# Attention pairs: one value half in a single run of four chunks, and full 128x128 transposes for the last keys and the tails of q and k

## The chip, the cores and the metric

The kernel runs on one core of one Trainium2 chip. The core has five engines that run at the same time and wait for each other by semaphores: TensorE (PE in the rows; its weight loads are PEld), VectorE (DVE), ScalarE (ACT), GpSimd (POOL) and SyncE (SP), which here issues the DMA transfers. The metric is the device time of one launch in microseconds (us); less is better.

## The reference

Three layers follow each other: an attention with a learned relative bias, a mixture of experts with one expert for each token, and a layer that takes the maximum of three projections. The change is in the first.

```
# q, k, v: (4 batches, 8 heads, 576 positions, 64)
scores = q @ k^T / sqrt(64) + bias[head]          # 576 x 576 for each batch and head
attn = exp(scores - max) / (sum + 1e-9)
x = attn @ v                                      # then (2304 tokens, 512) for the experts
out = max_of_three(experts(x))
```

All numbers are float32. Matmuls that need full precision use a high and a low part of each operand.

## The kernel before, in words

The 32 heads are worked on as 16 **pairs** of two heads, numbered here 0 to 15. The 576 queries of a head are four tiles of 128 and a **tail** of 64; the 576 keys are four chunks of 128 and the last 64. A pair takes five **steps**, 0 to 4. Steps 0 to 3 take one query tile of both heads each; step 4 takes the tails of both heads together.

The order in which instructions stand on each engine is the order in which the loop at the end of `attention` issues them; no scheduler moves them. In a step TensorE is given, in this order:

- the scores of this step (`scores`, L262): two products for each head, one that reads `qs` and `kh` and one that reads `qz` and `kl`;
- transposes that prepare a later pair (`prep`): its tails of q and k in step 0 (L176), its k in step 2 and its q in step 3 (L179); in some steps also a piece of work for the rows of a batch that is done (L425, L434, L445);
- a part of the product with the values (`av`, L409 and L405), into the one PSUM tile `oT`;
- the transposes of the probabilities that were normed one step before (`transpose_step`, L380 for the first 512 keys, L390 or L395 for the last 64).

The product with the values is made in two parts of the queries: j = 0 is the first 256 queries (steps 0 and 1), j = 1 the other 320. Table `AV` says which key chunks of which part stand in which step; chunk 4 is the last 64 keys of both heads in one full matmul (L405), the chunks 0 to 3 are two matmuls each, for one head on array columns 0 to 63 and for the other on 64 to 127.

The scores of the next pair need its q and k in a layout with both heads on all partitions. For that the transposed q is split into a high part by ScalarE (L194) and a low part by VectorE (L207), both in `hl`, and `move` issues six transfers on SP's queue: for each head two into `qs` (L216) and one into `qz` (L220). This stands in step 3; before them on the same queue, from step 2, stand four transfers into `kh` (L218) and two loads of a later k (L146). SP takes its queue strictly in order. The first use of `qs` and `qz` is in step 0 of the next pair, with step 4 between.

`norm_step` (L352 to L359) makes VectorE work out 1 over the sums, and GpSimd multiply the probabilities into `pr`. PSUM tiles of tag T (`pt`, `tp`, `tq` and others) share three buffers.

Of the kernel before, what the change touches and what calls it, by code (L numbers as in the profile page):

```python
# [12 lines left out]
F32 = mybir.dt.float32  # L13
# [4 lines left out]
ALU = mybir.AluOpType  # L18
# [4 lines left out]
P = 128  # L23
B, H, S, D = 4, 8, 576, 64
# [14 lines left out]
TAIL = S - 4 * P  # L39
# [57 lines left out]
def attention(tc, A, ident, x_dram, route, rpool, store):  # L97
    nc = tc.nc
    with ExitStack() as ctx:
# [4 lines left out]
        pl = ctx.enter_context(tc.tile_pool(name="pl", bufs=2, reuse_waits="tile"))  # L104
# [16 lines left out]
        HALF = (slice(0, D), slice(D, P))  # L121

        def load_pair(b, hp):

            t = {}
            for nm in ("q", "k"):
                t[nm] = pl.tile([P, 4, 2, D], F32, name=f"{nm}n", tag=f"{nm}n", bufs=1)
            t["tail"] = pl.tile([TAIL, 2, 2, D], F32, name="tn", tag="tn", bufs=1)
            t["v"] = pl.tile([P, 4, 2, D], F32, name="vn", tag="vn")


            t["qz"], t["vt"] = qz[hp % 2], vd[hp % 2]
            t["qs"] = pl.tile([P, 2, 512], F32R, name="qs", tag="qs")
            t["qd"] = qd[hp % 2]
            t["kh"] = pl.tile([P, 2, S], F32R, name="kh", tag="kh")
            t["kn"] = pl.tile([P, S], F32R, name="kn", tag="kn2")
            t["kl"] = pl.tile([P, S], F32R, name="kl", tag="kl")

            def load(nm):
                hs = slice(2 * hp, 2 * hp + 2)  # L140
                if nm == "tail":
                    for i, x in enumerate(("q", "k")):
                        nc.sync.dma_start(out=t[nm][:, i], in_=A[x][b, hs, 4 * P :].rearrange("h p d -> p h d"))
                    return
                for h in range(2):
                    nc.sync.dma_start(out=t[nm][:, :, h, :], in_=A[nm][b, 2 * hp + h, : 4 * P].rearrange("(c p) d -> p c d", p=P))  # L146
                if nm == "v":
                    for h in range(2):
                        nc.sync.dma_start(out=t["vt"][HALF[h], h, :], in_=A["v"][b, 2 * hp + h, 4 * P :])

            t["load"] = load
            return t

        st = [load_pair(*pairs[0])]
        mod = route.modality_rows()

# [15 lines left out]
        def prep(t, nm, pt):  # L172

            if nm == "tail":
                for i in range(2):
                    nc.tensor.transpose(pt[:, i * TAIL : (i + 1) * TAIL], t["tail"][:, i].rearrange("p h d -> p (h d)"), ident[:TAIL, :TAIL])  # L176
            else:
                for c in range(4):
                    nc.tensor.transpose(pt[:, c * P : (c + 1) * P], t[nm][:, c, :, :].rearrange("p h d -> p (h d)"), ident)  # L179
            return pt  # L180
# [130 lines left out]
        pTt = pb.tile([P, S], F32, name="pTt", bufs=1)  # L311
# [38 lines left out]
        def norm_step(mz, es):  # L350
            n = len(es)
            nc.vector.tensor_scalar(mz[:, 1, :n], mz[:, 1, :n], 1e-9, None, op0=ALU.add)  # L352
            nc.vector.reciprocal(mz[:, 1, :n], mz[:, 1, :n])
            pr = pb.tile([P, 2 * S], F32, name="pr", tag="pr", bufs=2)
            nc.gpsimd.tensor_scalar(pr[:, :S], es[0], mz[:, 1, 0:1], 1.0, op0=ALU.mult, op1=ALU.mult)  # L355
            if n == 2:
                r = mz[:, 1, 1:2]
                nc.gpsimd.tensor_scalar(pr[:, S : S + TAIL], es[1][:, 4 * P :], r, 1.0, op0=ALU.mult, op1=ALU.mult)
                nc.gpsimd.tensor_scalar(pr[:, S + TAIL :], es[1][:, : 4 * P], r, 1.0, op0=ALU.mult, op1=ALU.mult)  # L359
            return pr  # L360

        def ptile(t, h, it):
            if it < 2:
                return t["pT0"][:, h, :, it * P : (it + 1) * P]
            q = it * P - Q0
            return t["pT1"][:, h, :, q : q + (P if it < 4 else TAIL)]

        def transpose_step(t, it, pr):
            if it == 0:
                t["pT0"] = pb.tile([P, 2, 4, Q0], F32, name="pT0", tag="pT0", bufs=1)  # L370
                t["pTt"] = pTt
            if it == 2:
                t["pT1"] = pb.tile([P, 2, 4, Q1], F32, name="pT1", tag="pT1", bufs=1)
            for h in range(2):
                if it == 4 and h == 1:
                    break
                o = 0 if h == 0 else S + TAIL
                tp = ps.tile([P, 512], F32, name="tp", tag="T", bufs=3)
                for c in range(4):
                    nc.tensor.transpose(tp[:, c * P : (c + 1) * P], pr[:, o + c * P : o + (c + 1) * P], ident)  # L380
                if it < 4:
                    (nc.scalar.copy if h else nc.vector.tensor_copy)(ptile(t, h, it), tp.rearrange("p (c q) -> p c q", c=4))  # L382
                else:
                    for j in range(2):
                        (nc.scalar.copy if j else nc.vector.tensor_copy)(
                            ptile(t, j, it), tp.rearrange("p (c h q) -> p c h q", c=4, h=2)[:, :, j, :]
                        )
            tq = ps.tile([P, 512], F32, name="tq", tag="T", bufs=3)
            if it < 4:
                nc.tensor.transpose(tq[:, :P], pr[:, 4 * P : 4 * P + P], ident)  # L390
                nc.scalar.copy(t["pTt"][:, it * P : (it + 1) * P], tq[:, :P])
            else:
                for h in range(2):
                    hs = slice(h * D, h * D + D)
                    nc.tensor.matmul(tq[hs, :TAIL], pr[hs, 4 * P : S], ident[hs, hs], start=True, stop=True)  # L395
                nc.vector.tensor_copy(t["pTt"][:, 4 * P :], tq[:, :TAIL])

        def av(t, j, cs):
            if cs[0] == 0:
# [70 lines left out]

        PREP0 = ("tail", "k", "q", None, None)
        PREP = ("tail", None, "k", "q", None)
        AV = (((1, 0, (2, 3)),), ((1, 0, (4,)),), ((1, 1, (0, 1)),), ((1, 1, (2, 3, 4)),), ((0, 0, (0, 1)),))
        st = st + [None] * len(pairs)
        ROWS = (1, 2, 3, 4)
        LR = 4
# [11 lines left out]
        for i in range(len(steps) + 5):  # L488
            n, it = i // 5, i % 5
            cur = st[n] if n < len(pairs) else None  # L490
            last = st[n - 1] if n > 0 else None
            if cur:
                nm = (PREP if n else PREP0)[it]
                nxt = (st[n + 1], nm) if n + 1 < len(pairs) and nm else None
                mid = row_q and it in ROWS
                soft, pr = soft_step(cur, pairs[n][1], it, nxt, pend, row_q.pop(0) if mid else None, n >= len(pairs) - NP2, early.pop(0) if early else None)
            else:
                soft, pr = None, norm_step(*pend) if pend else None
            ready[i - 1] = pr
            pend = soft  # L500
            for back, j, cs in AV[it]:
                t = last if back else cur
                if t:
                    av(t, j, cs)
                    if 4 in cs:
                        evict_o(t, j)
            if 0 <= i - 2 < len(steps):
                m, jt = steps[i - 2]
                transpose_step(st[m], jt, ready.pop(i - 2))
            for f in EARLY.get((n, it), ()):  # L510
                f()
            if last and it == 3:
                b, hp = pairs[n - 1]
                if hp == NP2 - 1:
                    xTs = [st[n - NP2 + i2]["xT"] for i2 in range(NP2)]
                    if b == B - 1:
                        assert not ops
                        return lambda *allocs: batch_done(b, xTs, *allocs)
                    row_q += batch_done(b, xTs, talloc, lambda: px.tile([P, DM], F32, name="xr", tag="xr"))
            if n < len(pairs):  # L520
                if it == 0 and n + 2 < len(pairs):
                    st[n + 2] = load_pair(*pairs[n + 2])
                if it == 4 and n + 1 < len(pairs):
                    st[n + 1]["load"]("v")
                if nm and n + 2 < len(pairs):
                    st[n + 2]["load"](nm)
            if i > 7:
                next(gates, None)
            if i > 4:
                next(rconst, None)  # L530
# [1057 lines left out]
```

## Time and profile before

| what | value |
| --- | --- |
| median of 3 runs | 953.15 us (952.73 to 954.08) |
| the profiled execution | 953.03 us |
| its span, from first to last instruction | 951.3 us |
| TensorE busy | 923.9 us, 97% |
| VectorE, ScalarE, GpSimd busy | 547.5, 429.7, 206.3 us |

The profiled execution lies 1.7 us above its span and 0.1 us under the median. Matmuls are pipelined: a row's printed duration holds the time that a result needs to come out, so the cost of a group of matmuls on TensorE is read from its start to the start of the next group. Lines are those of the kernel before.

### The profile page before, as it was taken

How to read it: one execution, taken by the hardware profiler on the slowest of the kernel's cores; microseconds unless marked ns; L12 is line 12 of the kernel's file. 1: busy time of each engine (PE TensorE's matmuls, PEld its weight loads, DVE VectorE, ACT ScalarE, POOL GpSimd, SP SyncE). 2: the span in 40 equal slices, each digit the busy share in tenths (PEclk: the TensorE clock that was granted, in tenths of full speed). 3: DMA queues.
4: the chain of work that ended last, by engine and by line, in shares of the span. 5: the costliest groups of instructions: out<-in, count | busy, mean ns of one | idle time of the engine just before them, and what ended most of it. 6: DMA issues, size and time to landing. Idle time of an engine off the chain costs nothing. (4 is left out here: it accounts for less than half of the span.)

```text
span 951.3 us, 16953 instructions
## 1 busy us (share of the span) xinstructions
PE 923.9 (97%) x5667; PEld 723.8 (76%) x5667; DVE 547.5 (58%) x1267; ACT 429.7 (45%) x889; POOL 206.3 (22%) x350
## 2 busy tenths in 40 slices
PE   6989999999999999999999999999999999999996
PEld 3436777777777777788888887888888888888885
DVE  7976777877877886633355368525455365522221
ACT  6977766666767666322244256432111011122221
POOL 1004544453353451211112111110000000001112
PEclk9999999999999999999999999999999999999999
DMA  5976664664565564321234459314021121000111
GB/s 124 213 189 172 143 143 100 174 149 111 144 159 132 127 188 139 100 56 57 65 128 143 145 192 335 126 36 155 2 87 45 45 90 45 22 23 34 45 45 55
DMA packets 111037, 106.67 MB, mean 112 GB/s; under 512 B 69788, under 2 KB 79260, under 8 KB 110941
## 3 DMA queue, kind: packets, MB, share of 16 engines
q1 hardware_dynamic: 106140, 90.53, 34.7%
q0 software_dynamic: 4800, 14.97, 5.1%
q8 instruction: 47, 0.77, 0.4%
q14 instruction: 50, 0.40, 0.1%
HBM read 121.57 MB, written 14.96 MB: 144 GB/s over the span
## 5 line engine op out<-in xcount | busy, mean ns | idle before, releaser
L280 ACT ACTIVATE e<-e,mz 128x576 f32<-128x576 f32 x144 | 110.5, 770 | 34.4 <-DVE mz L268 34.4
L268 DVE CUSTOM_DVE_ANT_0 e<-s,bias 128x576 f32<-128x576 f32 x140 | 101.6, 756 | 18.1 <-PE s L262 17.0
L355 POOL TENSOR_SCALAR pr<-e,mz 128x576 f32<-128x576 f32 x80 | 59.7, 746 | 219.4 <-DMA bias<-ev 73.7
L380 PEld LDWEIGHTS tp<-ident,pr 128*128 128x128 f32 x576 | 64.0, 141 | 26.6 <-issue 10.0
L935 DVE TENSOR_TENSOR hl<-ht,hh 128x512 fp32r<-128x512 f32 x42 | 29.1, 692 | 94.6 <-ACT hh L934 85.5
L380 PE MATMUL tp<-ident,pr 128*128 128x128 f32 x576 | 79.2, 278 | 1.1 <-POOL pr L355 0.8
L1371 POOL DMA_INDIRECT out_dram<-res,tok x18 | 17.3, 959 | 287.3 <-ACT res L1370 287.3
L409 PE MATMUL oT<-pT,vn 128*64 128x320 f32 (+1 forms) x512 | 77.1, 418 | 0.2 <-ACT pT L382 0.2
L1341 PE MATMUL acc<-x2l,wrh 128*128 128x512 f32 x192 | 74.7, 389 | 0.0
L1341 PE MATMUL acc<-x2h,wrh 128*128 128x512 f32 x192 | 74.7, 389 | 0.0
L1341 PE MATMUL acc<-x2h,wrl 128*128 128x512 f32 x192 | 74.7, 389 | 0.0
L382 DVE COPY pT<-tp 128x512 f32<-128x512 f32 x64 | 44.2, 690 | 33.3 <-PE tp L380 32.7
L1347 DVE TENSOR_TENSOR h<-acc,h 128x512 f32<-128x512 f32 (+1 forms) x48 | 29.9, 622 | 55.5 <-PE acc L1341 55.0
L1473 PE MATMUL bp<-gt,w2d 128*32 128x512 f32 (+1 forms) x512 | 52.1, 432 | 9.3 <-ACT w2d L1459 7.4
L262 PE MATMUL s<-kh,qs 128*128 128x288 f32 x248 | 58.6, 318 | 0.1
L1010 POOL DMA_INDIRECT y_dram<-y,sca x21 | 21.5, 1026 | 160.1 <-ACT hh L934 145.1
L262 PE MATMUL s<-kl,qz 128*128 128x288 f32 x248 | 53.3, 296 | 1.2 <-DMA qz<-hl 0.9
L1540 DVE TENSOR_SCALAR gt<-tab,sc,nb 128x576 f32<-128x576 f32 x105 | 52.8, 580 | 1.1 <-PE bp L1473 0.7
L1473 PEld LDWEIGHTS bp<-gt,w2d 128*32 128x32 f32 x512 | 20.4, 112 | 39.2 <-issue 19.7
L409 PEld LDWEIGHTS oT<-pT,vn 128*64 128x64 f32 x512 | 32.5, 136 | 21.4 <-issue 3.9
L944 PE MATMUL yp<-wr,hh 128*128 128x512 f32 x120 | 47.0, 391 | 0.0
L946 PE MATMUL yp<-wr,hl 128*128 128x512 f32 x120 | 46.8, 390 | 0.0
(325 smaller groups left out, 2203.8 us busy)
## 6 DMA issues: line engine op xcount, KB each, us to landing
store<-in_moe_w_dram SPq DMA_DIRECT2D x160, 512.0 KB
bias<-ev SPq DMA_DIRECT2D x32, 288.0 KB
kh<-kn SPq DMA_DIRECT2D x64, 144.0 KB
raw<-in_moe_w_dram SPq DMA_DIRECT2D x18, 512.0 KB
qs<-hl SPq DMA_DIRECT2D x64, 128.0 KB
xr<-y_dram SPq DMA_DIRECT2D x18, 256.5 KB
kn<-in_k_dram SPq DMA_DIRECT2D x32, 128.0 KB
qn<-in_q_dram SPq DMA_DIRECT2D x32, 128.0 KB
```

Source lines behind the costliest of these rows:

```text
L262: nc.tensor.matmul(s[:, j, :SH], w, k[:, j * SH : (j + 1) * SH], start=i == 0, stop=i == len(terms) - 1)
L268: nc.vector.tensor_tensor_reduce(out=e.rearrange("p (a j) -> p a j", a=2), in0=s, in1=bt.rearrange("p (a j) -> p a j", a=2), op0=ALU.add, ...
L280: nc.scalar.activation(e, e, AF.Exp, bias=mz[:, 0, h : h + 1], scale=-1.0, accum_out=mz[:, 1, h : h + 1])
L355: nc.gpsimd.tensor_scalar(pr[:, :S], es[0], mz[:, 1, 0:1], 1.0, op0=ALU.mult, op1=ALU.mult)
L380: nc.tensor.transpose(tp[:, c * P : (c + 1) * P], pr[:, o + c * P : o + (c + 1) * P], ident)
L382: (nc.scalar.copy if h else nc.vector.tensor_copy)(ptile(t, h, it), tp.rearrange("p (c q) -> p c q", c=4))
L409: nc.tensor.matmul(oT[hs, :n], vt[:, c, h, :], t[f"pT{j}"][:, h, c, :], start=c == 0, stop=False)
L944: nc.tensor.matmul(out, ah, wh, start=first, stop=False)
L946: nc.tensor.matmul(out, al, wh, start=False, stop=last)
L1341: nc.tensor.matmul(a[:, :n], wt[:, m, ws], xt[:, c, :], start=c == 0 and k == 0, stop=c == KC - 1 and k == 2)
L1473: nc.tensor.matmul(out[c0 : c0 + 32, : hi - lo], ws, gs[g][:, lo:hi], start=True, stop=True, tile_position=(0, c0))
L1540: nc.vector.tensor_scalar(gt, x, s1, nb1, op0=ALU.mult, op1=ALU.max)
```

## The change

Four edits. In table `AV` the first part of the queries (j = 0, 256 queries) had its chunks 0 and 1 in step 4 of the pair itself and its chunks 2 and 3 in step 0 of the next; now all four stand in step 0 of the next pair, except for the last pair, where a second table keeps the old places. The tails of q and k of two heads are loaded into one tile of 128 partitions and transposed by one 128x128 transpose, where two of 64x128 were. The last 64 keys of step 4 are transposed by the same full 128x128 transpose as in the other steps, where two 64x64 matmuls were; the two halves that are wanted are then copied out by two copies. For that GpSimd writes the last 64 keys' probabilities a second time, beside the first. The part of 320 queries keeps its two runs.

```diff
-            t["tail"] = pl.tile([TAIL, 2, 2, D], F32, name="tn", tag="tn", bufs=1)
+            t["tail"] = pl.tile([2 * TAIL, 2, D], F32, name="tn", tag="tn", bufs=1)
...
-                        nc.sync.dma_start(out=t[nm][:, i], in_=A[x][b, hs, 4 * P :].rearrange("h p d -> p h d"))
+                        nc.sync.dma_start(out=t[nm][HALF[i]], in_=A[x][b, hs, 4 * P :].rearrange("h p d -> p h d"))
...
-                for i in range(2):
-                    nc.tensor.transpose(pt[:, i * TAIL : (i + 1) * TAIL], t["tail"][:, i].rearrange("p h d -> p (h d)"), ident[:TAIL, :TAIL])
+                nc.tensor.transpose(pt[:, :P], t["tail"].rearrange("p h d -> p (h d)"), ident)
...
             nc.gpsimd.tensor_scalar(pr[:, :S], es[0], mz[:, 1, 0:1], 1.0, op0=ALU.mult, op1=ALU.mult)
+            if n == 1:
+
+                nc.gpsimd.tensor_scalar(pr[:, S : S + TAIL], es[0][:, 4 * P :], mz[:, 1, 0:1], 1.0, op0=ALU.mult, op1=ALU.mult)
...
+            nc.tensor.transpose(tq[:, :P], pr[:, 4 * P : 4 * P + P], ident)
             if it < 4:
-                nc.tensor.transpose(tq[:, :P], pr[:, 4 * P : 4 * P + P], ident)
                 nc.scalar.copy(t["pTt"][:, it * P : (it + 1) * P], tq[:, :P])
             else:
                 for h in range(2):
                     hs = slice(h * D, h * D + D)
-                    nc.tensor.matmul(tq[hs, :TAIL], pr[hs, 4 * P : S], ident[hs, hs], start=True, stop=True)
-                nc.vector.tensor_copy(t["pTt"][:, 4 * P :], tq[:, :TAIL])
+                    nc.vector.tensor_copy(t["pTt"][hs, 4 * P :], tq[hs, hs])
...
-        AV = (((1, 0, (2, 3)),), ((1, 0, (4,)),), ((1, 1, (0, 1)),), ((1, 1, (2, 3, 4)),), ((0, 0, (0, 1)),))
+        AV = (((1, 0, (0, 1, 2, 3)),), ((1, 0, (4,)),), ((1, 1, (0, 1)),), ((1, 1, (2, 3, 4)),), ())
+
+        AV_END = {(15, 4): ((0, 0, (0, 1)),), (16, 0): ((1, 0, (2, 3)),)}
...
-            for back, j, cs in AV[it]:
+            for back, j, cs in AV_END.get((n, it), AV[it]):
```

On TensorE, step 4 of pair 1 and step 0 of pair 2 stood so before (`s` are scores, `oT` the product with the values, `tp` and `tq` transposed probabilities, `pt` with `tn` the transposed tails):

```order
L262 MATMUL s<-kl,qd_105 128x288 x2
L409 MATMUL oT<-pT_1374,vn 64x256 x4
L380 MATMUL tp<-ident,pr 128x128 x8
L390 MATMUL tq<-ident,pr 128x128
L262 MATMUL s<-kh,qs 128x288 x2
L262 MATMUL s<-kl,qz_106 128x288 x2
L262 MATMUL s<-kh,qs 128x288 x2
L262 MATMUL s<-kl,qz_106 128x288 x2
L176 MATMUL pt<-ident,tn 128x64 x2
L409 MATMUL oT<-pT_1374,vn 64x256 x4
```

In the changed kernel the same place on TensorE reads:

```order
L261 MATMUL s<-kl,qd_105 128x288 x2
L382 MATMUL tp<-ident,pr 128x128 x8
L391 MATMUL tq<-ident,pr 128x128
L261 MATMUL s<-kh,qs 128x288 x2
L261 MATMUL s<-kl,qz_106 128x288 x2
L261 MATMUL s<-kh,qs 128x288 x2
L261 MATMUL s<-kl,qz_106 128x288 x2
L175 MATMUL pt<-ident,tn 128x128
L410 MATMUL oT<-pT_1372,vn 64x256 x8
```

Four matmuls with the values moved from ahead of the next pair's scores to behind them, and the tails' two transposes became one.

In step 1 of the same pair TensorE had, from the last matmul with the values on:

```order
L405 MATMUL oT<-pTt,vd_109 128x256
L380 MATMUL tp<-ident,pr 128x128 x4
L395 MATMUL tq<-ident,pr 64x64 x2
L262 MATMUL s<-kh,qs 128x288 x2
L262 MATMUL s<-kl,qz_106 128x288 x2
```

and has now:

```order
L406 MATMUL oT<-pTt,vd_109 128x256
L382 MATMUL tp<-ident,pr 128x128 x4
L391 MATMUL tq<-ident,pr 128x128
L261 MATMUL s<-kh,qs 128x288 x2
L261 MATMUL s<-kl,qz_106 128x288 x2
```

The two 64x64 matmuls became a fifth full transpose; nothing else moved there.

## Rows read from the trace of the kernel before

**Rows 1.** The page: busy time of each engine, its share, instructions.

```profile
PE 923.9 (97%) x5667; PEld 723.8 (76%) x5667; DVE 547.5 (58%) x1267; ACT 429.7 (45%) x889; POOL 206.3 (22%) x350
```

**Rows 2.** TensorE's waits at the scores, 84 to 346 us: us, times.

```profile
  DMA qz<-hl: 3.2, 6
```

**Rows 3.** Timeline, TensorE, pair 1 step 3 to pair 2 step 2: start, us, group.

```profile
96.76 0.43 PE L262 MATMUL s<-kl,qz 128*128 128x288 f32 x2
97.03 0.60 PE L179 MATMUL pt<-ident,qn 128*128 128x128 f32 x4
97.56 1.30 PE L409 MATMUL oT<-pT,vn 128*64 128x320 f32 x8
98.78 0.81 PE L405 MATMUL oT<-pTt,vd 128*128 128x320 f32 x2
99.43 1.04 PE L380 MATMUL tp<-ident,pr 128*128 128x128 f32 x8
100.30 0.27 PE L390 MATMUL tq<-ident,pr 128*128 128x128 f32 x1
...
100.94 0.43 PE L262 MATMUL s<-kl,qd 128*128 128x288 f32 x2
101.30 1.08 PE L409 MATMUL oT<-pT,vn 128*64 128x256 f32 x8
102.31 1.09 PE L380 MATMUL tp<-ident,pr 128*128 128x128 f32 x8
103.24 0.27 PE L390 MATMUL tq<-ident,pr 128*128 128x128 f32 x1
103.27 0.52 PE L262 MATMUL s<-kh,qs 128*128 128x288 f32 x2
103.63 0.42 PE L262 MATMUL s<-kl,qz 128*128 128x288 f32 x2
103.88 0.42 PE L262 MATMUL s<-kh,qs 128*128 128x288 f32 x2
104.39 0.53 PE L262 MATMUL s<-kl,qz 128*128 128x288 f32 x2
104.85 0.34 PE L176 MATMUL pt<-ident,tn 64*128 64x64 f32 x2
105.12 1.08 PE L409 MATMUL oT<-pT,vn 128*64 128x256 f32 x8
...
108.66 0.60 PE L380 MATMUL tp<-ident,pr 128*128 128x128 f32 x4
...
109.81 0.42 PE L262 MATMUL s<-kl,qz 128*128 128x288 f32 x2
```

**Rows 4.** Timeline, SP's queue, the transfers of k and q for pair 2.

```profile
94.42 3.18 SPq L218 DMA_DIRECT2D kh<-kn  x4
...
102.03 0.60 SPq L220 DMA_DIRECT2D qz<-hl  x1
```

**Rows 5.** Timelines, all engines, where pairs 5 and 15 begin.

```profile
153.87 0.59 SPq L220 DMA_DIRECT2D qz<-hl  x1
...
157.67 0.43 PE L262 MATMUL s<-kl,qz 128*128 128x288 f32 x2
...
342.12 0.59 SPq L220 DMA_DIRECT2D qz<-hl  x1
...
344.97 0.43 PE L262 MATMUL s<-kl,qz 128*128 128x288 f32 x2
```

**Rows 6.** TensorE's waits, 84 to 372 us: us, times, longest.

```profile
PE tq L390 <- DVE xr L449: 1.2, 4, 0.5
```

**Rows 7.** Timeline, VectorE, pair 3 from step 1 to step 2.

```profile
127.73 0.21 DVE L396 COPY pTt<-tq 128x64 f32<-128x64 f32 x1
128.23 0.17 DVE L352 TENSOR_SCALAR mz<-mz 128x2 f32<-128x2 f32 x1 [0.28 <-ACT e L280]
```

**Rows 8.** GpSimd's 128x64 norm: ns min/median/max, first and last start.

```profile
L358 POOL TENSOR_SCALAR pr<-e,mz x64: 308/317/321, 77.5 to 359.1; 128x64 f32<-128x64 f32 x64
```

## The prediction

> **What bounds the kernel now.** I read four views in this order. The page first: TensorE is busy for 97% of the span, the next engine for 58% [rows 1], so time goes only where TensorE's own order gets shorter or where it starts to wait. Then TensorE's waits in the attention: between 84 and 346 us it sat at the scores six times, 3.2 us in all, and each time for a transfer into `qz` [rows 2]. Then its timeline around one such wait [rows 3], in which a group's cost is its start to the next start. Last SP's queue for the same pair [rows 4].
>
> The reader is to see one thing in the last two. In pair 2 the fourth group of scores should follow the third after 0.25 to 0.27 us, as elsewhere in the rows, at 104.15; it starts at 104.39. The last of the six transfers of q left SP's queue at 102.03 + 0.60 = 102.63, so 1.76 us pass from there to TensorE's start [rows 3, 4]. SP had been at that queue since 94.42, when k was transposed and split. So at the head of this pair the bound is not TensorE but a chain of transfers: k and q transposed in steps 2 and 3, SP's queue, landing, fourth group of scores. Step 4 and the front of step 0 are what TensorE does meanwhile.
>
> How long TensorE is late or early there is its slack. With 1.76 us after the end of the sixth issue, pair 5 has 157.67 - (154.46 + 1.76) = 1.45 us to spare and pair 15 has 344.97 - (342.71 + 1.76) = 0.50 [rows 5]. Done the same way for all: pairs 1, 2, 3, 4, 8 and 11 have none (they are the six waits), 7, 12, 14 and 15 have 0.30, 0.35, 0.14 and 0.50, and 5, 6, 9, 10 and 13 have 1.45, 1.21, 1.07, 1.21 and 1.45, because work for the rows of a finished batch stands between.
>
> **The change part by part.** First what each edit is worth in TensorE's order alone.
>
> The run of the first half. From the last scores of step 4 to `tq` it is 103.24 - 100.94 = 2.30 us. Without the run, the two scores take 0.27 (96.76 to 97.03) and eight transposes 0.87 (99.43 to 100.30): 1.14. Step 4 loses 1.16 [rows 3]. In step 0 four matmuls are added to a run that is there. A run of four costs 1.22 with 320 columns (97.56 to 98.78) and 1.01 with 256 (101.30 to 102.31); 64 columns are 0.21, so 256 are 0.84 and 0.17 is fixed [rows 3]. The added half costs 0.84 if the fixed part is paid once, 1.01 if it is paid again. I take 0.84: within the run nothing changes shape. Alone this edit gives 0.32 in each of 15 pairs.
>
> The tails. From the last scores to the values it is 0.36 (100.94 to 101.30 shows what a change from full to half columns costs after scores, 0.09 more than 0.27) plus 0.27 (104.85 to 105.12), so 0.63. New: 0.27, one transpose of 0.87 / 8 = 0.11, and 0.09 for the change of shape (97.03 to 97.56 is 0.53 for four transposes of 0.11): 0.47. It gives 0.16 in 15 pairs [rows 3].
>
> The last 64 keys. From the four transposes of step 1 to the second group of scores it is 109.81 - 108.66 = 1.15. New: four at 0.11, then 0.03 and 0.36 as behind a full transpose (103.24, 103.27, 103.63): 0.83. It gives 0.32 in 16 pairs [rows 3].
>
> Sum, if TensorE never waited more: 15 x 0.32 + 15 x 0.16 + 16 x 0.32 = 12.3 us.
>
> Now where each part lies. The 1.16 us that leave step 4 are ahead of the fourth group of scores; the 0.84 that come, and the 0.16 and 0.32 that go, are behind it. Neither k's transpose nor q's, which start the chain, stands behind any of it in the same pair, so the landing stays where it is against them, and TensorE, which takes its queue in order, arrives 1.16 earlier and waits. Behind it then wait the tails' transpose, the whole longer run and everything after. A pair without slack therefore gets longer by 0.84 - 0.16 - 0.32 = 0.36 us; one with slack s gets 0.36 - min(s, 1.16), and 0.10 more where the wait is new, since the group after a wait costs 0.46 in place of 0.36 (104.39 to 104.85 against 100.94 to 101.30) [rows 3].
>
> - Six pairs without slack: 6 x 0.36 = +2.2.
> - Pairs 7, 12, 14 and 15: +0.16, +0.11, +0.32 and +0.12 (15 has no tails to gain from): +0.7.
> - Pairs 5, 6, 10 and 13: 4 x -0.80 = -3.2; pair 9: 0.36 - 1.07 + 0.10 = -0.6.
> - Four times TensorE already waits in step 2 or 3 at `tq` for VectorE's copy of rows [rows 6]. What step 1 saves just ahead of these is waited there: 4 x 0.32 = +1.3.
> - Pair 15's last keys, where nothing of this follows: -0.3.
>
> The sum is +0.1 us, on the profiled execution's own 953.03: 953.1. The median lies 0.12 over that execution; I leave it at 953.1 us, no change.
>
> Costs set at nothing. GpSimd's added norm takes 0.32 us [rows 8], 16 times, 5.1 us; GpSimd is busy for 22% [rows 1], and its product is read a step later; uncovered it would be those 5.1. VectorE gets two 64x64 copies for one of 128x64 that took 0.21; the second costs 0 to 0.21, and the 0.28 that VectorE then sits idle cover it [rows 7]. The two loads of the tails stay two; their other partitions I cost at 0, within 0.1 either way. The first pair's tails in the setup are not on TensorE's bound.
>
> The rows show that a change of shape costs 0.09 going into a run of half columns and more at the small 64x64 form. [...] The rows also show the wait at `qz` with the work that now moves behind it. [...]
>
> **The rivals.**
>
> *Full gain.* The chain of transfers gets earlier too, or the slack is larger than 1.76 us from the last issue suggests, and the 12.3 stay: 940.7. For it speaks that SP waits for ScalarE's split of k at its start, and so follows TensorE. Against it: it follows k's transpose, which stands before step 4, and all six waits end at a landing [rows 2]. Half of it would be 947.
>
> *Slower: VectorE takes over between steps 1 and 2.* Step 1 gets 0.32 shorter for TensorE and up to 0.21 longer for VectorE, whose next norm must wait for ScalarE's exponentials anyway. If VectorE falls behind there, the 0.32 are lost in the other 11 pairs (+3.5) and 0.21 are waited in 15 (+3.2): 959.8. It decides once VectorE's added copy outlasts its idle 0.28 us [rows 7]; a copy of 0.21 does not, unless pieces of the routing stand there, which they do in some pairs only.
>
> *The change does not do what it says.* It is said to be for the half with 320 queries; in the table, and in TensorE's order, the merged run is that with 256, and the 320 stay as they were. The working above is for what the code does, so this has no time of its own.
>
> **How the numbers follow.** Forecast 0.62, full or half gain 0.20, VectorE 0.18. The forecast's own range is 950.5 to 956.5: up by 15 x 0.17 = 2.5 if the added half pays its fixed part, and by 0.9 for another transfer that comes late by chance; down by 1.3 if the waits at `tq` do not take the savings, and by 0.9 if the slack of the nine free pairs is 0.1 larger. For 8 times in 10 I take 948 to 957.5, which leaves out most of the full gain and the worst of VectorE. A measurement of this kernel tells from no change what is over 0.2%, 1.9 us. Of the forecast 0.05 lies below that and 0.09 above: faster 0.25, same 0.48, slower 0.27.
>
> **What would show it.** In the changed profile TensorE's waits for `qz` or `qs` at the scores would be some 11 in place of six, each up to 1.2 us, and 10 us or more in all; the fourth group of scores would still start about 1.76 us behind the end of SP's sixth issue of q. Step 4 would show eight transposes 0.27 us behind the scores; step 0 a run of 16 rows over 1.85 us; step 1 0.83 us from `tp` to the second scores. The forecast is wrong if these waits stay near 3 us (then the gain is real), or if new waits for VectorE at `s`, `pt` or `tq` sum to over 3 us (then it is slower).

## The result and the profile after

The kernel after takes 962.9 us (median of 8 runs, 958.88 to 967.35) against 954.23 for the kernel before beside it: ratio 1.009, 95% interval 1.0071 to 1.0109. It is slower by 0.9%, where no change, 953.1 us in a range of 948 to 957.5, was forecast. Its eight runs stand in two groups, four from 958.88 to 960.02 us with a mean granted TensorE clock of 0.996 to 0.999 and four from 965.78 to 967.35 with 0.991 to 0.994, and by the lower four alone it is 0.6%. The profiled execution took 960.02 us with a span of 958.2. Its attention stage, from the first scores to the first matmul of the experts, takes 372.79 - 73.93 = 298.9 us against 367.37 - 74.95 = 292.4, so 6.4 of the 7 us lie there; 1.5 us of the 298.9 are a fall of TensorE's clock ahead of the pairs compared below (last section).

First the page of the kernel after, busy time of each engine, as in [rows 1].

```profile
PE 921.3 (96%) x5603; PEld 723.3 (75%) x5603; DVE 550.2 (57%) x1283; ACT 430.5 (45%) x889; POOL 212.7 (22%) x366
```

TensorE has 2.6 us less to do and the kernel is 7 us longer: it waits. Second, what its idle time at the scores ended with, 84 to 346 us (us, times), as in [rows 2].

```profile
  issue: 4.0, 6
  DVE mz L352: 3.5, 4
  DMA qz<-hl: 2.9, 11
  DMA qs<-hl: 2.1, 4
```

Where six waits had stood at `qz`, eleven stand there and four at `qs`. A wait that this view puts down to another engine can be a transfer's too. TensorE's timeline at the place of [rows 3] has one, at 102.50.

```profile
100.01 0.44 PE L261 MATMUL s<-kl,qd 128*128 128x288 f32 x2
100.28 1.04 PE L382 MATMUL tp<-ident,pr 128*128 128x128 f32 x8
101.15 0.27 PE L391 MATMUL tq<-ident,pr 128*128 128x128 f32 x1
101.18 0.51 PE L261 MATMUL s<-kh,qs 128*128 128x288 f32 x2
101.53 0.43 PE L261 MATMUL s<-kl,qz 128*128 128x288 f32 x2
102.50 0.50 PE L261 MATMUL s<-kh,qs 128*128 128x288 f32 x2 [0.54 <-DVE mz L351]
103.10 0.53 PE L261 MATMUL s<-kl,qz 128*128 128x288 f32 x2
103.47 0.27 PE L175 MATMUL pt<-ident,tn 128*128 128x128 f32 x1
103.67 1.95 PE L410 MATMUL oT<-pT,vn 128*64 128x256 f32 x16
105.55 1.09 PE L382 MATMUL tp<-ident,pr 128*128 128x128 f32 x8
...
108.08 0.60 PE L382 MATMUL tp<-ident,pr 128*128 128x128 f32 x4
108.51 0.27 PE L391 MATMUL tq<-ident,pr 128*128 128x128 f32 x1
108.54 0.51 PE L261 MATMUL s<-kh,qs 128*128 128x288 f32 x2
108.89 0.42 PE L261 MATMUL s<-kl,qz 128*128 128x288 f32 x2
```

The steps of the prediction are there: eight transposes 0.27 us behind the scores, a run of 16 rows that takes 105.55 - 103.67 = 1.88, 0.81 from `tp` to the second scores of step 1. The third and fourth groups of scores wait. The third is put down to VectorE's `mz`, which the scores don't read; the buffer that they write had been read out by VectorE at 100.59 to 101.35. For the same pair SP's queue, as in [rows 4], shows when the last transfers of q were issued.

```profile
99.48 1.23 SPq L215 DMA_DIRECT2D qs<-hl  x2
100.75 0.60 SPq L219 DMA_DIRECT2D qz<-hl  x1
```

From the end of the last, 101.35, to the fourth group at 103.10 it is 1.75 us, where it was 1.76. From the end of the issues into `qs`, 100.71, to the third group it is 1.79, so that wait is a transfer's too. The four groups take 0.87 from the first start to the fourth where nothing is late (137.78 - 136.91 below); pair 2 takes 103.10 - 101.18 = 1.92, so 1.05 of waiting. Done so for pairs 2 to 15 it is 9.2 us, and was 2.2 before. These are called the head waits.

The stretch from the fourth group of scores of pair 2 to that of pair 15 (13 pairs) is a cleaner measure than a whole run, in which setup and experts differ by a microsecond or two (ahead of the first scores 74.95 and 73.93 us in the profiles of before and after, behind the attention 951.3 - 367.37 = 583.9 and 958.2 - 372.79 = 585.4): before 344.97 - 104.39 = 240.6 us, after 349.41 - 103.10 = 246.3. Below it is called the stretch, and the part of it from one pair's fourth group to that of the next is the period that ends at the next.

### The profile page after: what moved, and what is told of

Read it like the earlier page. It is cut to its first block, busy times and chain, and to the rows that moved or that the text cites. A ratio compares the mean times of both kernels' runs of the same rounds, so it can differ in the third digit from the quotient of the medians.

```text
span 958.2 us, 16870 instructions
## 1 busy us (share of the span) xinstructions
PE 921.3 (96%) x5603; PEld 723.3 (75%) x5603; DVE 550.2 (57%) x1283; ACT 430.5 (45%) x889; POOL 212.7 (22%) x366
## 5 line engine op out<-in xcount | busy, mean ns | idle before, releaser
L410 PE MATMUL oT<-pT,vn 128*64 128x320 f32 (+1 forms) x512 | 73.5, 415 | 0.2 <-DVE pT L387 0.2
```

The costliest lines, as they stand in the source:

```text
L410: nc.tensor.matmul(oT[hs, :n], vt[:, c, h, :], t[f"pT{j}"][:, h, c, :], start=c == 0, stop=False)
```

## The experiments

Each ratio is to runs of the kernel before taken beside it (medians 953.17 us for the first four rows, 954.09 for the next four, 953.76 for the last four), so rows of different groups are compared by their ratios. A stretch is that of one profiled execution.

| kernel | median us | ratio to before (95%) | stretch us |
|---|---|---|---|
| run of values alone | 961.58 | 1.0083 (1.0062 to 1.0104) | 246.8 |
| tails and last keys | 951.27 | 0.9975 (0.9963 to 0.9987) | 237.3 |
| last keys alone | 954.83 | 1.0011 (0.9996 to 1.0026) | 241.2 |
| tails alone | 950.74 | 0.9973 (0.9960 to 0.9986) | 238.1 |
| before, k and q one step earlier | 954.11 | 0.9998 (0.9984 to 1.0011) | 240.0 |
| the same, run of values moved | 953.67 | 0.9998 (0.9981 to 1.0016) | 241.0 |
| after, k and q one step earlier | 956.70 | 1.0031 (1.0011 to 1.0051) | 242.0 |
| last keys, second copy on ScalarE | 952.67 | 0.9990 (0.9973 to 1.0006) | 238.7 |
| earlier, run moved in plain pairs | 951.85 | 0.9984 (0.9971 to 0.9998) | 238.6 |
| built from what held | 947.99 | 0.9947 (0.9932 to 0.9962) | 235.3 |
| that, with the last keys | 948.73 | 0.9943 (0.9925 to 0.9960) | 235.2 |
| after again | 961.34 | 1.0080 (1.0066 to 1.0093) | 248.4 |

**The run of values alone.**

```diff
-        AV = (((1, 0, (2, 3)),), ..., ((0, 0, (0, 1)),))
+        AV = (((1, 0, (0, 1, 2, 3)),), ..., ())
+        AV_END = {(15, 4): ((0, 0, (0, 1)),), (16, 0): ((1, 0, (2, 3)),)}
```

> The kernel before with the moved run of values alone (tails and last keys stay as they were). Theory A, the moved run is the cost: TensorE loses 1.16 us of work ahead of the fourth group of scores and waits there for q's transfers instead, and the longer run of step 0 lies behind that wait. By the terms of the prediction this is +0.84 in the six pairs without slack and +2 in all in the others less some 1.4 in those with work for rows: about +6, 957 to 962 us, with waits for qz or qs in eleven pairs or more, 10 us of TensorE in all. Theory B, VectorE and the three T buffers are the cost, through the last keys' second copy: then the moved run alone is near 953, 951 to 955.

Measured 1.0083: theory A. This edit alone costs as much as the whole change, and the scores wait for `qs` and `qz` 17 times. The head waits are 8.1 us, 5.9 more than before, and the stretch is 6.2 longer.

**Tails and last keys.** Against the kernel after:

```diff
-        AV = (((1, 0, (0, 1, 2, 3)),), ..., ())
-        AV_END = {(15, 4): ((0, 0, (0, 1)),), (16, 0): ((1, 0, (2, 3)),)}
+        AV = (((1, 0, (2, 3)),), ..., ((0, 0, (0, 1)),))
```

> The kernel after with the run of values put back (full transposes of the tails and of the last 64 keys alone). Theory A: both edits lie behind the wait for q's transfers and ahead of k's and q's transposes, so their 0.16 and 0.32 us a pair are kept but for 1.3 at the copies of rows: 953 - 6 = 947, 945 to 950 us. Theory B: VectorE's second copy and GpSimd's added norm make TensorE wait at the scores of step 2 and at the T buffers: 955 to 961 us.

Measured 951.27: faster, against theory B, but 4 us short of the 947 of theory A.

**Last keys alone.**

```diff
+                nc.gpsimd.tensor_scalar(pr[:, S : S + TAIL], es[0][:, 4 * P :], ...)
+            nc.tensor.transpose(tq[:, :P], pr[:, 4 * P : 4 * P + P], ident)
-                nc.vector.tensor_copy(t["pTt"][:, 4 * P :], tq[:, :TAIL])
+                    nc.vector.tensor_copy(t["pTt"][hs, 4 * P :], tq[hs, hs])
```

> The kernel before with the full transpose of the last 64 keys alone. Theory A: 16 x 0.32 less up to 1.3 waited at the copies of rows, 948 to 950 us. Theory B: the second copy takes 0.24 us in which VectorE had stood idle 0.28 at most, TensorE waits for VectorE in step 2 of most pairs, 954 to 959 us.

Measured 954.83, in theory B's range, ratio 1.0011 with 1 inside the interval: this is where theory A's 4 us are missing. The timeline of VectorE from step 1 to step 2 of pair 3, as in [rows 7], shows why.

```profile
128.10 0.45 DVE L398 COPY pTt<-tq 64x64 f32<-64x64 f32 x2
128.60 0.17 DVE L352 TENSOR_SCALAR mz<-mz 128x2 f32<-128x2 f32 x1
```

Two copies take 0.45 where one took 0.21. One 64x64 copy takes 204 to 229 ns in the profile of after (median 218 of 32 copies) and one 128x64 copy 214 to 217 in that of before (median 216 of 16), so here a copy of 64 partitions costs what a copy of 128 does. The idle 0.28 are gone.

In a plain pair the edit gives 0.20 a period (pair 12, 17.18 before and 16.98 here), not 0.32: the gap from k's transposes to q's grows from 132.16 - 128.30 = 3.86 to 132.32 - 128.33 = 3.99. In a pair with rows it costs. These are pairs 5, 9 and 13, in which the rows of a finished batch are transposed in steps 2 to 4 (`xr_p`; the last two in the next pair) and copied out; in step 4 of pairs 4, 8 and 12 stand the logits of that batch (`lp`). In pairs with rows VectorE had no idle time at this place, as its timeline of before at pair 5, step 1 to 2, shows:

```profile
164.25 0.41 DVE L385 COPY pT<-tp 128x256 f32<-128x256 f32 x1
164.58 0.21 DVE L396 COPY pTt<-tq 128x64 f32<-128x64 f32 x1
164.76 0.17 DVE L352 TENSOR_SCALAR mz<-mz 128x2 f32<-128x2 f32 x1
...
167.37 0.68 DVE L449 COPY xr<-xr_p 128x512 f32<-128x512 f32 x1
```

and with the last keys alone:

```profile
164.67 0.45 DVE L398 COPY pTt<-tq 64x64 f32<-64x64 f32 x2
165.15 0.17 DVE L352 TENSOR_SCALAR mz<-mz 128x2 f32<-128x2 f32 x1
...
167.84 0.68 DVE L451 COPY xr<-xr_p 128x512 f32<-128x512 f32 x1
```

The copy of rows, which frees a T buffer, starts 0.47 later, and with it TensorE, which waits for that buffer at `tq` before and here:

```profile
168.57 0.33 PE L392 MATMUL tq<-ident,pr 128*128 128x128 f32 x1 [0.20 <-DVE xr L451]
```

It stood at 168.11 before; of the 0.46, 0.09 is that this pair began later. The periods that end at pairs 6, 10 and 14 get longer by 0.37, 0.39 and 0.44. The head waits are 3.4 us for 2.2, which takes another 1.2 from this edit's gain.

**Tails alone.**

```diff
-                    nc.tensor.transpose(pt[:, i * TAIL : (i + 1) * TAIL], t["tail"][:, i]..., ident[:TAIL, :TAIL])
+                nc.tensor.transpose(pt[:, :P], t["tail"].rearrange("p h d -> p (h d)"), ident)
```

> The kernel before with the full transpose of the tails alone. Both theories: 15 x 0.16 = 2.4 us less, 950.7, 949.5 to 953 us; if the tile that now holds the tails of q and k on 128 partitions costs in its loads or copies, nothing or a little more than before.

Measured 950.74, as forecast; the period that ends at pair 12 falls from 17.18 to 17.04. The stretches of the three edits alone change by +6.2, -2.5 and +0.6, which sums to +4.3; together they are at +5.7, and at +7.8 in the repeat below, 1.6 of which are a fall of TensorE's clock (last section).

**k and q one step earlier.** The question is now whether the moved run costs only because of the transfers.

```diff
-        PREP = ("tail", None, "k", "q", None)
+        PREP = ("tail", "k", "q", None, None)
```

> The kernel before with k transposed in step 1 and q in step 2 (one step earlier each), nothing else. Theory A, the landing of q's transfers bounds the head of a pair: they now leave SP's queue some 3 us earlier, the waits at the scores for qz and qs go (3.2 us in the profile of before), 949 to 951 us. Rival, VectorE: the low parts of k and q now fall where copies of rows and norms stand, and TensorE waits for these in place of the transfers: 953 or more.

Measured 954.11, ratio 0.9998: the time is the rival's, and the mechanism of both came true. The waits at `qs` and `qz` are gone, a plain pair takes 17.09 us each time, and the periods that end at pairs 6, 10 and 14 take 0.5 to 0.7 more (20.19 for 19.66 at pair 6): TensorE waits three times at `xr_p` for VectorE, 1.8 us in all, where before had one such wait of 0.3. The slack at pair 4, in a timeline of all engines:

```profile
133.37 0.59 SPq L220 DMA_DIRECT2D qz<-hl  x1
...
136.91 0.51 PE L262 MATMUL s<-kh,qs 128*128 128x288 f32 x2
...
137.78 0.43 PE L262 MATMUL s<-kl,qz 128*128 128x288 f32 x2
```

With 1.76 behind the issue's end, 133.96, TensorE has 2.06 us to spare.

**The same with the run of values moved.** Both edits, the run and the earlier transposes.

```diff
+        AV = (((1, 0, (0, 1, 2, 3)),), ..., ())
+        PREP = ("tail", "k", "q", None, None)
```

> The kernel before with the moved run of values and with k and q transposed one step earlier. Theory A: without the wait for q's transfers the moved run is worth its 0.32 us in TensorE's order in each of 15 pairs, so this is 3 to 5 us below the same kernel with the run where it was (the experiment with the earlier transposes alone), where without the earlier transposes the run cost 8. Rival, the moved run costs by itself (T buffers in step 4, or the longer run of step 0): it stays 4 us or more above that kernel.

Measured 953.67 against 954.11: the 8 us are gone, so it was the wait for the transfers that cost them. By the stretch the run costs 0.9 here, and 6.2 without the earlier transposes. The gain of 3 to 5 did not come, so theory A was only part of it. A plain pair, one without logits or rows, does gain 0.30 at pair 8 (17.09 to 16.79), and 0.17 to 0.20 in the four others, where it or the pair before still waits a little for a landing. Pairs with logits lose 0.17 (18.20 to 18.37) and pairs with rows 0.4 to 0.7. TensorE in step 4 of pair 4, which has logits, with the run in its old place:

```profile
152.03 1.18 PE L425 MATMUL lp<-xT,wg 128*32 128x512 f32 x16
153.14 1.08 PE L409 MATMUL oT<-pT,vn 128*64 128x256 f32 x8
154.15 1.09 PE L380 MATMUL tp<-ident,pr 128*128 128x128 f32 x8
155.08 0.27 PE L390 MATMUL tq<-ident,pr 128*128 128x128 f32 x1
```

and with the run moved:

```profile
153.46 1.18 PE L425 MATMUL lp<-xT,wg 128*32 128x512 f32 x16
154.57 1.41 PE L380 MATMUL tp<-ident,pr 128*128 128x128 f32 x8
155.82 0.27 PE L390 MATMUL tq<-ident,pr 128*128 128x128 f32 x1
```

with ScalarE beside it:

```profile
154.62 0.58 ACT L428 COPY lt<-lp 128x512 f32<-128x512 f32 x1 [1.20 <-PE lp L425]
155.10 0.22 ACT L428 COPY ltt<-lp 128x64 f32<-128x64 f32 x1
```

The eight transposes go into two T buffers. The two tiles of logits hold two of the three, and the second of the two is free only when ScalarE's copy of the first tile ends, at 154.62 + 0.58 = 155.20. From `tp` to `tq` it is 1.25 us, where it was 0.93. So the run that left had covered 0.32 of this, and the move saves (155.08 - 152.03) - (155.82 - 153.46) = 0.69 us where 1.16 was forecast. In pairs with rows it is the tile of rows. TensorE in step 4 of pair 5, with the run in its old place:

```profile
172.80 0.60 PE L445 MATMUL xr_p<-ident,xT 128*128 128x128 f32 x4
...
175.27 0.27 PE L390 MATMUL tq<-ident,pr 128*128 128x128 f32 x1
175.30 0.51 PE L262 MATMUL s<-kh,qs 128*128 128x288 f32 x2
```

and with the run moved:

```profile
174.40 0.60 PE L445 MATMUL xr_p<-ident,xT 128*128 128x128 f32 x4
174.84 1.04 PE L380 MATMUL tp<-ident,pr 128*128 128x128 f32 x8
176.24 0.33 PE L390 MATMUL tq<-ident,pr 128*128 128x128 f32 x1 [0.36 <-DVE xr L449]
176.45 0.50 PE L262 MATMUL s<-kh,qs 128*128 128x288 f32 x2
```

From `xr_p` to `tq` it is 1.84 us. Before the move it is 2.47, so 0.63 is saved where 1.16 was forecast; up to the scores behind, 2.05 for 2.50, it is 0.45.

**After, with k and q one step earlier.** Against the kernel after:

```diff
-        PREP = ("tail", None, "k", "q", None)
+        PREP = ("tail", "k", "q", None, None)
```

> The kernel after with k and q transposed one step earlier. Theory A: all three edits count in TensorE's order, 12.3 us less what the last keys lose to VectorE (they gave nothing alone): 942 to 947 us. Rival, as for the moved run: 955 us or more.

Measured 956.70: the rival's range, though the ratio fell from 1.009 to 1.0031, without a change to any of the three edits. Theory A is wrong, and with the transfers out of the way (head waits 2.0 us) the three edits still cost 0.3%. The period that ends at pair 6 takes 20.91 here and 20.59 without the two kinds of full transposes, a plain one 16.69 and 16.79: 0.10 gained of the 0.48 that the two are worth in TensorE's order.

**Last keys, second copy on ScalarE.**

```diff
-                    nc.vector.tensor_copy(t["pTt"][hs, 4 * P :], tq[hs, hs])
+                    (nc.scalar.copy if h else nc.vector.tensor_copy)(t["pTt"][hs, 4 * P :], tq[hs, hs])
```

> The kernel before with the full transpose of the last 64 keys, the second of its two 64x64 copies on ScalarE in place of VectorE. Theory V, the last keys gave nothing alone because VectorE falls behind by that second copy (0.13 us between k's and q's transposes in a plain pair, 0.4 to 0.5 in pairs with rows): it now gives most of its 16 x 0.32, 949 to 951.5 us. Rival, the gain is lost to the T buffers or GpSimd's added norm whoever copies: 953.5 to 956 us, as with both on VectorE.

Measured 952.67, ratio 0.9990 against 1.0011 with both copies on VectorE. The intervals overlap by a little, and 952.67 lies between the two ranges, so the whole time leans to theory V but does not settle it. VectorE's timeline at the place of [rows 7] shows the cover back:

```profile
127.21 0.20 DVE L398 COPY pTt<-tq 64x64 f32<-64x64 f32 x1
127.70 0.17 DVE L352 TENSOR_SCALAR mz<-mz 128x2 f32<-128x2 f32 x1 [0.29 <-ACT e L280]
```

The periods that end at pairs 6, 10 and 14 are 19.65, 19.77 and 20.56 again (before 19.66, 19.77 and 20.57, with both copies on VectorE 20.03, 20.16 and 21.01). So the cost in pairs with rows is the second copy on VectorE, since GpSimd's added norm stands in both; a gain of 0.32 did not come there either.

**Earlier, the run moved in plain pairs alone.**

```diff
+        for p in (4, 5, 8, 9, 12, 13, 15):
+            AV_END[p, 4] = ((0, 0, (0, 1)),)
+            AV_END[p + 1, 0] = ((1, 0, (2, 3)),)
```

> k and q transposed one step earlier, and the moved run of values only in the nine pairs 0, 1, 2, 3, 6, 7, 10, 11 and 14, where no logits or rows of a finished batch stand in step 4; in the six pairs 4, 5, 8, 9, 12 and 13 the run stays in step 4. Theory A2, without the wait for transfers the moved run gains 0.30 us in a plain pair and loses 0.2 to 0.7 where step 4's transposes find the T buffers still full of logits or rows: 9 x 0.30 = 2.7 us below the earlier transposes alone, 950.5 to 952.5 us, and periods of 16.8, 18.2 and 20.2 us in plain pairs, pairs with logits and pairs with rows. Rival, the run gives nothing anywhere: 953.5 to 955 us.

Measured 951.85, in the range of theory A2, but the gain over the earlier transposes alone is 1.4 us of stretch and 0.0014 of the ratio, half of the 2.7, and the two intervals overlap. The periods that I named were wrong for two kinds: the longer run falls into the pair with logits (19.06) and the saved one into the pair behind the rows (17.10). Over the periods that end at pairs 4 to 7 that is 16.88 + 19.06 + 20.20 + 17.10 = 73.24 against 17.09 + 18.20 + 20.19 + 18.26 = 73.74, two times 0.25.

**Built from what held.** Tails, the run moved as above, k and q earlier but in pairs 5, 9 and 13.

```diff
-                nm = (PREP if n else PREP0)[it]
+                nm = (PREP if n in (5, 9, 13) else PREP0)[it]
```

> A version built from what held: full transpose of the tails, the moved run in the nine plain pairs, k and q one step earlier except in the three pairs with rows (5, 9, 13), no change to the last keys. Theory A2: the 950.7 us of the tails alone, less 9 x 0.30 for the runs and 1 to 2 for waits at the transfers: 945.5 to 948 us. Rival, the moved run costs beyond what the periods show: 950 us or more.

Measured 947.99 at the upper end of what was expected; ratio 0.9947, interval 0.9932 to 0.9962. It beats both kernels. Its head waits are 0.6 us, where before has 2.2.

**That with the last keys added.**

```diff
+                    (nc.scalar.copy if h else nc.vector.tensor_copy)(t["pTt"][hs, 4 * P :], tq[hs, hs])
```

> The version before this one with the full transpose of the last 64 keys added, its second copy on ScalarE. Theory V: 1 to 3 us less than that version, 943.5 to 946.5 us. Rival, with k's low part one step earlier VectorE and ScalarE stand as close as before and the last keys give nothing again: equal or slower, 946 to 949 us.

Measured 948.73, the same as without. Theory V's 1 to 3 us did not come. The plain period that ends at pair 8 is shorter (16.47 for 16.64), but the head waits are 2.1 us for 0.6.

**After again.** No edit.

> The kernel after, unchanged, beside the others: its eight runs were at 959 to 960 us four times and at 966 to 967 four times. If the upper group comes from this kernel, it comes again (some runs near 966); if it came from that chip, all runs are at 958 to 962 us. The ratio to before stays 1.006 to 1.010 either way.

Measured 959.83 to 962.62, ratio 1.0080. No run near 966 came back in six, so that group does not belong to every set of this kernel's runs. What made it is not shown; its mean clock is lower (0.991 to 0.994).

## Why the prediction was wrong

- *The bound.* Right. The transfers of q end 1.75 us behind their last issue, TensorE waits there instead of working, and 9.2 us of waits came where "10 us or more" were said; single ones reached 1.63 where "up to 1.2" was said. That it is this wait which costs the run its 8 us is shown by the earlier transposes, which take the 8 us away.
- *The three edits in TensorE's order.* Right within 0.03: 0.30 for the run in a plain pair that waits nowhere (0.32), 0.14 for the tails (0.16); the last keys' 0.32 stands in the timeline (0.81 to the second scores, 0.83 forecast).
- *Pairs without slack.* Pairs 3, 4, 8 and 11 were to lose 1.4 together and lost 2.4; pairs 7, 12, 14 and 15 were to lose 0.7 and lost 2.0. Pair 8 was misread: by the prediction's own rule it had 213.59 - (210.46 + 1.76) = 1.37 of slack, and its wait in the profile of before was one late landing, 3.13 us behind the issue. In after it came at 1.80, and pair 8 got 0.56 shorter; pairs 3, 4 and 11 lost 2.9.
- *The step that failed: "one with slack s gets 0.36 - min(s, 1.16)".* It was to give 3.8 us back in pairs 5, 6, 9, 10 and 13. They got 1.3 us longer: the stretch was to change by 1.4 + 0.7 - 3.8 + 1.3 = -0.4 and changed by +5.7. The run of values alone shows how much of these 5.1 us is this step: by the same rule, 0.84 - min(s, 1.16), it was to give 1.4 in these five pairs, and it cost 1.2. The slack was there, but TensorE does not come 1.16 earlier: step 4's transposes find the T buffers full of logits or rows, and 0.45 to 0.69 is what the move saves there. I had priced it against the transfers alone. The other half of the 5.1 lies with the full transposes.
- *The second step that failed: "the second costs 0 to 0.21, and the 0.28 that VectorE then sits idle cover it".* The copy took 0.24, and in the pairs with rows there is no idle time at that place: rows 7 are from a plain pair. The last keys were to give 0.32 in 16 pairs, less 1.3; alone they gave nothing that can be measured. This is the rival "VectorE takes over", whose mechanism I had and whose condition I read from one pair. That its 959.8 us lies near the measured time is luck: the run of values alone, with VectorE's copies as before, takes 961.58. Why the last keys gave nothing in the version built from what held, with the second copy on ScalarE, is only in part seen.
- *The waits at `tq` for rows.* "4 x 0.32 = +1.3" was right in kind. These waits grew from 1.2 us to 1.6 with the last keys alone, four times in both. In after they are 2.2 in six, as the waits of TensorE show beside [rows 6]; the two that are new come with the moved run, which alone has six, 1.9 us.

```profile
PE tq L391 <- DVE xr L450: 2.2, 6, 0.8
```

- *The sum.* In the 13 periods of the stretch the terms of the prediction make +4.4 for the run, -1.9 for the tails and -2.9 for the last keys with the waits at `tq`; alone they measure +6.2, -2.5 and +0.6. So the last keys are the largest miss, 3.5 us. Together the edits are at +5.7, and at +6.2 in the repeat without its fall of clock, where the three alone sum to +4.3. What the 1.4 or more are made of is only in part seen: a late VectorE moves q's transpose (by 0.13 us in a plain pair with the last keys alone) and with it the landing that the moved run waits for. No run separates that from the scatter between two profiles of one kernel, 0.5 us here.

## What to carry to other kernels

Before work is moved off a place, list everything that it covers there: here not one landing of transfers but also a landing of logits and rows in three PSUM buffers, and each was worth a part of what the move should have saved. Read a cover in every kind of iteration, not in the plainest: the 0.28 us that hid a copy in a plain pair did not exist where rows are copied. An edit that costs in some iterations and gains in others is best made only in the others: the run moved in plain pairs alone, with the transfers a step earlier and the full transpose of the tails, is faster than both kernels (947.99 us, ratio 0.9947).

## What was not expected of the hardware

A copy of half the partitions was not cheaper: 64x64 took 0.20 us on VectorE, 128x64 took 0.21.

TensorE's clock can fall in one run of a kernel and not in another at the same place. In the profile of after it was granted half (0.50) from 79.5 to 82.9 us, right behind 0.90 us of waiting at `tq`; the columns are PE, PEld, DVE, ACT and POOL busy, granted clock, DMA share, GB/s.

```profile
79.50:82.90 3.40, 3.40 (x17) 3.38 (x17) 2.51 (x8) 2.25 (x7) 1.71 (x3) 0.50 0.87 208
80.86 1.91 PE L382 MATMUL tp<-ident,pr 128*128 128x128 f32 x8
```

The same kernel in the repeat has the same wait there and keeps its full clock (1.00 on average from 70 to 90 us):

```profile
79.03 0.33 PE L391 MATMUL tq<-ident,pr 128*128 128x128 f32 x1 [0.90 <-DVE hl L206]
...
80.25 1.04 PE L382 MATMUL tp<-ident,pr 128*128 128x128 f32 x8
```

The eight transposes took 1.91 and 1.04, and from this `tq` to the scores of `qd` it is 82.64 - 79.03 = 3.61 and 81.15 - 79.03 = 2.12 us: the half clock cost 1.5. It lies ahead of the stretch. The repeat has its own fall inside the stretch, right behind a wait for `qs` of the kind that the moved run makes longer:

```profile
122.95:126.30 3.35, 3.35 (x17) 1.85 (x18) 1.43 (x5) 2.17 (x7) 0.00 (x0) 0.50 0.56 122
```

```profile
122.10 0.50 PE L261 MATMUL s<-kh,qs 128*128 128x288 f32 x2 [0.79 <-DMA qs<-hl]
...
123.46 3.34 PE L410 MATMUL oT<-pT,vn 128*64 128x256 f32 x16
```

From the fourth group of this pair, 3, to the transposes behind the run it is 126.73 - 122.66 = 4.07 us, and 124.32 - 121.88 = 2.44 in the profile of after: 1.6 lost.

Issues on SP's queue are late in a pattern. In the profile of after, 84 to 346 us, nine issues took over 0.9 us where the median is 0.59, and beside each a fetch of instructions (16 KB, another DMA queue) starts less than 0.2 us away. Five of them are transfers into `kh`, which q's transfers follow: those for pair 3 took 3.61 us, those for pair 2 2.43. That the fetch is the cause is not shown.
